# Attention block on one core: half of x transposed by DMA, contraction in chunks of 128, K in four tiles, the last projection beside the last unit, row bounds from bits

## The chip, the core and the metric

The kernel runs on one core of a Trainium2 chip. The core has a matrix engine (TensorE, PE in the profile), a vector engine (VectorE, DVE), an engine for element functions (ScalarE, ACT), a general engine (GpSimd, POOL) and one that mostly issues transfers (SyncE, SP). They run side by side, each through its own instructions in order, and wait for each other by semaphores. Matrix products land in PSUM, eight banks of 128 rows by 512 numbers of 32 bits; everything else lies in SBUF. Transfers are issued by SP, ACT or POOL and carried out by 16 DMA engines that all issuers share. The metric is the time of one execution on the device in microseconds (us).

## The reference

Input x has 2048 rows of 448 numbers in bf16. The weights wqkv make queries, keys and values of it, for 16 heads of 28 numbers each; wo projects the result back.

```python
qkv = (x @ wqkv).reshape(B, S, 3, H, Dh).transpose(2, 0, 3, 1, 4)   # B=1, S=2048, H=16, Dh=28
q, k, v = qkv[0], qkv[1], qkv[2]
scores = einsum("bhqd,bhkd->bhqk", q, k) * Dh ** -0.5
p = softmax(scores, axis=-1)
o = einsum("bhqk,bhkd->bhqd", p, v)
out = o.transpose(0, 2, 1, 3).reshape(B, S, D) @ wo
```

So there are 16 x 2048 x 2048 exponentials, 67 million, and they are the bulk of the element work.

## The kernel before

**Layout.** The 16 heads are taken in four groups g of four. A head takes 32 rows: 28 of data and four spare ones. XT holds x transposed, in four blocks of 512 rows, with the 448 columns as four chunks of 112 on the partitions (CK, line 83). WP holds the weights of one group, padded from 28 to 32 columns a head (pad_w, line 193, on DVE). QA is Q transposed for a group and a chunk c of 512 queries; KA is K transposed for a group, one tile of 2048 columns (line 116); VA is V with columns of ones, so that the product with V also gives the softmax's denominator in row 28.

**Tiles and units.** A tile (g, c, j, i) is 128 keys by 512 queries of one head. There are 1024; three in a row make a unit, 342 in all, the last with one tile only. The scores of a unit go to three PSUM banks, in turn spA and spB (emit_S, line 788). ACT takes the exponential of the unit in one instruction (emit_exp, line 806, L808). For some units ACT takes two tiles and DVE the third: DVE makes an exponential out of the score's bits (class Pair: bits at L825 for each tile, then mant, expo, square, line and rest for two tiles together), in three summands. PE multiplies each with V and sums over the keys in the bank o_ps (emit_wave, line 860, L871). A set is one group and one chunk of queries, 16 in all.

**The bound.** So that no exponential overflows, each row of scores is lowered by a bound, |q| max|k|. It sits in spare rows of QA, against rows of 1 and -1 in KA. For it, squares of K are summed over a head by a matmul with a mask (k_norm_mm, line 222) and reduced to a maximum (k_norm_max, line 225: four times a group, then once more over the four). q_root (line 256) makes the root on ACT, as a logarithm and an exponential of half of it (lz at L258, root at L260), and SP copies it into the row 31 of each head of QA, one transfer a chunk. For the first chunk the bound is made by separate instructions (lines 331 to 347).

**The start** (lines 134 to 349). SP loads x in four blocks and the greater part of the weights, ACT the weights of the first group. Nine matmuls on zeros warm PE up. PE transposes all of x by the identity (L292, 16 a block), DVE and ACT copy the results out of PSUM (evac_x, L298), then follow K of the first group, the norms and the first chunk of Q. The order is written out by hand.

**The middle.** From line 375 on a planner written in Python decides the order when the program is built. It steps through time with fixed durations (DUR, EXP_STEP), has one list of candidates per engine (pick_a, pick_p, pick_v), chooses which units give a tile to DVE (choose_d), and hands PE further tasks in gaps: K, Q, V and norms of the next group (k_task, kn_task, q_task, qn_task, v_task), and the output projection of finished rows (oproj_task, L491). Tasks use the bank misc. The resulting log is emitted in order; in_program_order keeps every engine to it.

**The end.** Once all scores are issued and the second last exponential is done, emit_fin (line 877) issues 12 matmuls (L883): the last 512 output rows, four blocks of 128, times the projection of the first three groups. Then come the last products with V, the division by the denominator in two halves (turned, line 911: transpose by 32 x 32 blocks, reciprocal, multiply, transpose back), the last group's projection (L974), copies out of PSUM and the stores.

**Row order.** Row r of x goes to partition r // 16 of the tiles (`x3 = x2.rearrange("(p t) c -> p t c", t=NKT)`), and the output's rows in the same way (out_perm); attention does not depend on the order of keys.

## Time and profile before

| | |
|---|---|
| median of 3 runs | 427.89 us (426.48 to 428.4) |
| profiled execution, time | 425.97 us |
| profiled execution, span | 424.2 us, first to last instruction |
| mean granted TensorE clock | 0.978 |
| first exponential (L808) starts | 19.93 us |
| last exponential (L808) starts, lasts | 412.68 us, 0.93 us |
| ACT busy from 60 to 120 us | 59.97 us |
| DVE busy from 60 to 120 us | 59.39 us |
| bits instructions on DVE (L825) | 170, mean 0.69 us |

All numbers but the median come from one profiled execution. A span counts from the first instruction to the last; the execution's time is a little longer. Where a line of the profile reads "L808 ACT ACTIVATE pt<-spA 128x1536 ... x171 | 243.0, 1421 | 4.2 <-PE spA L791 4.2", the engine ACT executed 171 instructions of line 808, which read tile spA and wrote pt, were busy for 243.0 us in all, 1421 ns each on average, and ACT stood idle 4.2 us just before them, for most of it until PE's instruction of line 791 was done. Lines of one instruction after another on ACT overlap: an exponential of 1536 columns lasts 1.45 us or more, and the next one starts 1.34 us after it. In the chain of waits, a line has the start, the length and what the end hung on at that time; "x4" are four instructions in a row. A waits line reads: who waited, for whom, us in total, times, longest.

### The profile page before, as it was taken

What the parts mean: (1) busy time and instruction counts of PE and PEld (TensorE: products, weight loads), DVE (VectorE), ACT (ScalarE), POOL (GpSimd) and SP (SyncE); (2) the same over time, 40 slices, a digit from 0 to 9 for tenths busy, and PEclk for the clock granted to TensorE, in tenths of its full rate; (3) what the DMA queues carried; (4) which work ended last, traced back from release to release, by engine and by line L of the source; (5) the groups of instructions that cost most, each with busy time, mean ns of one, the idle gap of its engine ahead of it and who ended that gap; (6) DMA issues with size and microseconds to landing.
All of it is one profiled execution on the core that took longest, in us unless ns stands there. A gap on an engine that the chain in (4) does not pass through costs nothing.

```text
span 424.2 us, 7645 instructions
## 1 busy us (share of the span) xinstructions
PE 352.1 (83%) x2968; PEld 126.1 (30%) x2968; DVE 387.3 (91%) x808; ACT 402.7 (95%) x366; POOL 4.4 (1%) x26
## 2 busy tenths in 40 slices
PE   8588888887888888888788888888897888898883
PEld 5243222222333222223333222222323322222221
DVE  4758999999999999999999999999989999999943
ACT  4599999999999999999999999999999999999991
POOL 4000000000000000000000000000000000000000
PEclk9989999999999999999999999999869999999997
DMA  8300000000000000000000000000000000001011
GB/s 247 80 0 3 2 23 5 2 27 0 14 17 26 2 4 25 2 25 2 29 2 19 10 1 27 1 15 14 29 2 3 25 1 23 24 11 34 11 34 43
DMA packets 10923, 9.16 MB, mean 22 GB/s; under 512 B 4940, under 2 KB 8840, under 8 KB 10888
## 3 DMA queue, kind: packets, MB, share of 16 engines
q1 hardware_dynamic: 9672, 8.25, 6.6%
q10 hardware_dynamic: 1216, 0.44, 0.4%
q8 instruction: 23, 0.38, 0.4%
q14 instruction: 12, 0.10, 0.1%
HBM read 6.59 MB, written 1.93 MB: 20 GB/s over the span
## 4 chain that ended last, share of the span: by engine, by line
ACT 66%; issue 14%; PE 11%; DVE 8%; ACTq 0%
ACT pt L808 64%; PE o_ps L871 3%; DVE bits L825 2%; PE spA L791 1%; PE spB L791 1%; PE K L301 1%; ACT lz L258 1%; DVE nsq L841 1%; PE K L202 1%; PE misc L268 1%; DVE rest L849 1%; ACT root L260 1%; DVE mant L830 1%; PE misc L234 1%; PE Ta L292 1%
## 5 line engine op out<-in xcount | busy, mean ns | idle before, releaser
L808 ACT ACTIVATE pt<-spA 128x1536 bf16<-128x1536 f32 (+1 forms) x171 | 243.0, 1421 | 4.2 <-PE spA L791 4.2
L808 ACT ACTIVATE pt<-spB 128x1024 bf16<-128x1024 f32 (+1 forms) x171 | 241.4, 1412 | 0.5 <-PE spB L791 0.5
L871 PE MATMUL o_ps<-pt,VA 128*32 128x512 bf16 x854 | 133.6, 391 | 0.2
L791 PEld LDWEIGHTS <-KA 32*128 32x128 bf16 x1024 | 51.7, 91 | 165.7 <-issue 122.1
L791 PE MATMUL spB<-QA,KA 32*128 32x512 bf16 x511 | 68.0, 385 | 31.2 <-ACT pt L808 27.9
L791 PE MATMUL spA<-QA,KA 32*128 32x512 bf16 x513 | 68.1, 387 | 30.9 <-ACT pt L808 24.7
L825 DVE TENSOR_SCALAR bits<-spB 128x512 int16<-128x512 f32 x86 | 59.0, 686 | 4.3 <-PE spB L791 3.1
L825 DVE TENSOR_SCALAR bits<-spA 128x512 int16<-128x512 f32 x84 | 57.6, 686 | 4.9 <-PE spA L791 3.9
L849 DVE TENSOR_TENSOR rest<-line,bits 128x1024 bf16<-128x1024 bf16 x85 | 57.8, 680 | 0.2
L841 DVE TENSOR_TENSOR nsq<-mant 128x1024 bf16<-128x1024 bf16 x85 | 57.9, 681 | 0.0
L871 PEld LDWEIGHTS <-VA 128*32 128x32 bf16 x1364 | 35.0, 94 | 71.8 <-issue 66.6
L871 PE MATMUL o_ps<-bits,VA 128*32 128x512 bf16 x170 | 54.0, 392 | 0.0
L871 PE MATMUL o_ps<-expo,VA 128*32 128x512 bf16 x170 | 37.0, 392 | 0.0
L830 DVE TENSOR_SCALAR mant<-bits 128x1024 int16<-128x1024 int16 x85 | 35.6, 418 | 0.2
L845 DVE TENSOR_SCALAR line<-nsq 128x1024 bf16<-128x1024 bf16 x85 | 35.4, 416 | 0.3
L835 DVE TENSOR_SCALAR expo<-bits 128x1024 int16<-128x1024 int16 x85 | 35.6, 419 | 0.0
L871 PE MATMUL o_ps<-rest,VA 128*32 128x512 bf16 x170 | 34.8, 396 | 0.0
L268 PEld LDWEIGHTS <-XT 112*128 112x128 bf16 x256 | 15.6, 101 | 11.9 <-issue 11.9
L268 PE MATMUL misc<-WRAW,XT 112*128 112x128 bf16 x208 | 18.8, 227 | 0.0
L234 PE MATMUL misc<-XT,WP 112*128 112x512 bf16 x60 | 18.5, 400 | 0.2
L238 DVE TENSOR_SCALAR QA<-misc,qmask,offs 128x512 bf16<-128x512 f32 x15 | 12.1, 805 | 4.0 <-PE misc L234 4.0
L202 PE MATMUL misc<-XT,WP 112*128 112x512 bf16 x48 | 14.3, 384 | 0.3 <-DVE KPART L226 0.3
(87 smaller groups left out, 195.4 us busy)
## 6 DMA issues: line engine op xcount, KB each, us to landing
rr<-scr SPq DMA_DIRECT2D x12, 256.0 KB
xs<-in_x_dram SPq DMA_DIRECT2D x4, 448.0 KB
out_dram<-osb SPq DMA_DIRECT2D x14, 112.0 KB
WRAW<-in_wqkv_dram SPq DMA_DIRECT2D x2, 290.5 KB
WRAW<-in_wqkv_dram SPq DMA_DIRECT2D x1, 392.0 KB
WO<-in_wo_dram SPq DMA_DIRECT2D x16, 24.5 KB
QA<-root SPq DMA_DIRECT2D x15, 4.0 KB
out_dram<-osb ACTq DMA_DIRECT2D x2, 112.0 KB
```

The source lines that it names most:

```text
L202: nc.tensor.matmul(out=ps, lhsT=WP[1][g][:, cc, :], rhs=XT[sc][:, cc, :], start=(cc == 0), stop=(cc == CC - 1))
L234: nc.tensor.matmul(out=ps, lhsT=WP[0][g][:, cc, :], rhs=XT[c][:, cc, :], start=(cc == 0), stop=(cc == CC - 1))
L268: nc.tensor.matmul(out=ps[:, t * P:(t + 1) * P], lhsT=XT[b][:, cc, t * P:(t + 1) * P], rhs=wcols(2, cc, g * HG, HG), start=(cc == 0), stop ...
L791: nc.tensor.matmul(out=sp[:, t * QW:(t + 1) * QW], lhsT=KA[g][HP * i:HP * (i + 1), j * P:(j + 1) * P], rhs=QA[g][c][HP * i:HP * (i + 1), : ...
L808: e = nc.scalar.activation(out=pt[:, 0:n * QW], in_=sps[u][:, 0:n * QW], func=ACT.Exp, scale=LN2, bias=-BIAS * LN2)
L825: return nc.vector.tensor_scalar(out=self.bits[:, k * QW:(k + 1) * QW], in0=ps, scalar1=0.0, scalar2=128.0, op0=ALU.max, op1=ALU.mult)
L830: nc.vector.tensor_scalar(out=self.m[:], in0=self.bits[:], scalar1=0x7F, scalar2=0x3F80, op0=ALU.bitwise_and, op1=ALU.bitwise_or)
L835: nc.vector.tensor_scalar(out=self.e[:], in0=self.bits[:], scalar1=0x7F80, scalar2=None, op0=ALU.bitwise_and)
L841: nc.vector.tensor_tensor(out=self.q[:], in0=m, in1=m, op=ALU.mult)
L845: nc.vector.tensor_scalar(out=self.l[:], in0=self.q[:], scalar1=CB, scalar2=CE, op0=ALU.mult, op1=ALU.add)
L849: nc.vector.tensor_tensor(out=self.c[:], in0=self.l[:], in1=self.bits[:].bitcast(BF16), op=ALU.mult)
L871: nc.tensor.matmul(out=o_cur[s][HP * i:HP * (i + 1), :], lhsT=VA[g][j // XB][:, j % XB, HP * i:HP * (i + 1)], rhs=rhs, start=(first_pv[(s, ...
```

## The change

- **x.** Blocks 2 and 3 of x (rows 1024 to 2047) are no longer loaded and transposed by PE. Two DMA transposes for each write XT directly (load_xt): one for columns 0 to 383 and one for columns 320 to 447. They stand on SP's queue behind the loads of blocks 0 and 1. Rows of blocks 0 and 1 are spread over the partitions as before, those of blocks 2 and 3 lie in natural order, in the output too (out_rows).
- **Chunks of 128.** The four chunks begin at columns 0, 128, 256 and 320. The last overlaps the third by 64, and the first 64 rows of its weights are zero (three memsets on POOL). Each load of weights is split in two transfers. WO is loaded by 4 transfers instead of 16.
- **K.** KA is four tiles of 512 columns per group. In the start, K1 and K2 are copied out by ACT (k_evac_act), and the steps of the start stand in a new order.
- **Bounds.** The root is made on DVE from the bits of the squared norms (q_bits): half of the sum of two numbers' bits is about the bits of the root of their product. KBITS adds half of the bits of max|k|^2 and a constant that keeps the bound high enough. The norms of K of groups 1 to 3 go to one bank by four matmuls, with one maximum and four tiny DVE steps (transpose of 32 x 32 blocks, maximum, scale, transpose back) for four maxima.
- **End.** The first two of the four last blocks get their projection of three groups in banks of the last unit's own tile, once all scores are issued and the exponential two before the last is done; the other two after the last product with V. The division transposes once in full and then works in two halves; ACT copies three blocks out, DVE one.

The two orders of instructions on the engines differ in number as follows: bits 168 for 170, with 84 pairs for 85; maxima of norms in the middle (KPART and kt from misc) 3 for 12; transposes of x on PE 32 for 64; transfers issued by ACT at the start 4 for 2; by SP up to and with WO 16 for 23.

```diff
+WARM2 = 0
-    CK = D // CC
+    CK = 128
+    C3 = D - CK
+    CEIL = 12.0
+    MINUS_ROOT = 0.5 * 127 * 2.0 ** 23 + 0.0435 * 2 ** 23 - 2.0 ** 31
...
-    KA = [big.tile([P, S], BF16, name=f"KA{g}") for g in range(2)] * 2
+    KA = [[big.tile([P, QW], BF16, name=f"KA{g}_{c}") for c in range(NQC)] for g in range(2)] * 2
...
     def load_w(t, eng, a, b):
-        eng.dma_start(out=WRAW[t][:, :, a:b], in_=wq3[:, :, t * D + a:t * D + b])
+        cols = slice(t * D + a, t * D + b)
+        eng.dma_start(out=WRAW[t][:, 0:CC - 1, a:b],
+                      in_=wqkv[0:(CC - 1) * CK, cols].rearrange("(cc p) n -> p cc n", p=CK))
+        eng.dma_start(out=WRAW[t][CK // 2:CK, CC - 1, a:b], in_=wqkv[D - CK // 2:D, cols])
...
+    def load_xt(b, eng):
+        rows = x2[b * QW:(b + 1) * QW]
+        eng.dma_start_transpose(out=XT[b][:, 0:CC - 1, :], in_=rows[:, 0:(CC - 1) * CK])
+        eng.dma_start_transpose(out=XT[b][:, CC - 1:CC, :], in_=rows[:, C3:D])
+
+    for t in range(3):
+        nc.gpsimd.memset(WRAW[t][0:CK // 2, CC - 1, :], 0.0)
     load_x(0, nc.sync)
     load_w(1, nc.scalar, 0, W0)
     load_x(1, nc.sync)
     load_w(0, nc.scalar, 0, W0)
-    load_x(2, nc.sync)
-    load_x(3, nc.sync)
+    load_xt(2, nc.sync)
+    load_xt(3, nc.sync)
     load_w(2, nc.sync, 0, D)
     load_w(1, nc.sync, W0, D)
     load_w(0, nc.sync, W0, D)
...
+    nc.gpsimd.memset(kt[0][:], 0.0)
+    nc.gpsimd.memset(kt[2][:], 0.0)
...
-    def q_root(ps, g, cs):
-        lz = wk.tile([P, QW], F32, name="lz")
-        nc.scalar.activation(out=lz[:], in_=ps, func=ACT.Ln, bias=epscol[:, 0:1], scale=KMAX2[g][:, 0:1])
-        su = wk.tile([P, QW], BF16, name="root")
-        nc.scalar.activation(out=su[:], in_=lz[:], func=ACT.Exp, scale=0.5)
+    def q_bits(ps, g, cs):
+        su = wk.tile([P, QW], I16, name="root")
+        nc.vector.tensor_scalar(out=su[:], in0=ps.bitcast(I32), scalar1=2.0 ** -17, scalar2=KBITS[g][:, 0:1],
+                                op0=ALU.mult, op1=ALU.add)
...
+    def k_bits(g):
+        nc.vector.tensor_scalar(out=KBITS[g][:], in0=KMAX2[g][:, 0:1].bitcast(I32), scalar1=2.0 ** -17,
+                                scalar2=CEIL, op0=ALU.mult, op1=ALU.add)
...
+        def k_evac_act(ps, sc):
+            nc.scalar.activation(out=KA[0][sc][:], in_=ps, func=ACT.Identity, scale=kmask[:, 0:1], bias=ones[:, 0:1])
...
         pad_w(nc.vector, 1, 0)
         transposes(1)
         evac_x(1)
+        pad_w(nc.vector, 0, 0)
         k_mm(bank["K0"], 0, 0, ALLC)
         k_sq_act(bank["K0"], 0, 0)
-        pad_w(nc.vector, 0, 0)
-        transposes(2)
-        evac_x(2)
         k_evac(bank["K0"], 0, 0)
         k_mm(bank["K1"], 0, 1, ALLC)
         k_sq_act(bank["K1"], 0, 1)
-        transposes(3)
-        evac_x(3)
+        q_mm(bank["Ta0"], 0, 0, ALLC)
+        q_sq_act(bank["Ta0"], 0, 0)
+        k_norm_mm(bank["Tb0"], 0, 0)
+        k_norm_max(bank["Tb0"], 0, 0)
         k_mm(bank["K2"], 0, 2, ALLC)
...
-        nc.scalar.activation(out=lk[:], in_=KMAX2[0][:], func=ACT.Ln, bias=epscol[:, 0:1])
-        nc.scalar.activation(out=ak[:], in_=lk[:], func=ACT.Exp, scale=0.5)
...
-        k_evac(bank["K2"], 0, 2)
+        k_evac_act(bank["K1"], 1)
+        k_evac_act(bank["K2"], 2)
         k_evac(bank["K3"], 0, 3)
...
-    for h in range(H):
-        g, i = divmod(h, HG)
-        nc.sync.dma_start(out=WO[HP * i:HP * i + Dh, g, :], in_=wo[h * Dh:(h + 1) * Dh, :])
+    for i in range(HG):
+        nc.sync.dma_start(out=WO[HP * i:HP * i + Dh, :, :],
+                          in_=wo.rearrange("(g i e) n -> i e g n", g=G, i=HG)[i])
...
+            red = add_v(lambda: nc.vector.reduce_max(out=kt[0][:, 0:1], in_=tk.tile[:], axis=AX.X), "kred", [mm_], 2)
+            steps_ = [lambda: nc.vector.transpose(out=kt[1][:], in_=kt[0][:]),
+                      lambda: nc.vector.reduce_max(out=kt[3][:], in_=kt[1][:, Dh:HP], axis=AX.X),
+                      lambda: nc.vector.tensor_scalar(out=kt[2][:, Dh:HP], in0=kt[3][:].to_broadcast([P, NQC]),
+                                                      scalar1=MARG2, scalar2=None, op0=ALU.mult),
+                      lambda: nc.vector.transpose(out=kt[4][g][:], in_=kt[2][:])]
...
-            op = Op(lambda: q_root(tk.tile[:], g, cs), 0, [mm] + [("kmax", g, sc) for sc in range(NQC)] * (g > 0))
-            alist.append(op)
+            kb = add_v(lambda: k_bits(g), "tiny", [("kmax", g)] if g else [], 3, margin=0.03)
+            op = add_v(lambda: q_bits(tk.tile[:], g, cs), "evac", [mm, kb], 2)
...
     def emit_fin():
-        fin = sp_tile(NU)
-        fin_banks.extend([fin[:, 0:QW], fin[:, QW:2 * QW], fin[:, 2 * QW:3 * QW], misc_tile()[:]])
-        for tq in range(XB):
-            for g in range(G - 1):
-                nc.tensor.matmul(out=fin_banks[tq][:, 0:D], lhsT=OT[g][CL][:, tq * P:(tq + 1) * P],
-                                 rhs=WO[:, g, :], start=(g == 0), stop=False)
+        sp = sps[NU - 1]
+        fin_banks.extend([sp[:, QW:2 * QW], sp[:, 2 * QW:3 * QW]])
+        for tq in range(2):
+            fin_mm(tq)
+
+    def fin_mm(tq):
+        for g in range(G - 1):
+            mm = nc.tensor.matmul(out=fin_banks[tq][:, 0:D], lhsT=OT[g][CL][:, tq * P:(tq + 1) * P],
+                                  rhs=WO[:, g, :], start=(g == 0), stop=False)
+            if tq < 2:
+                beside.append(mm)
...
     o_ps = o_cur[NSET - 1]
+    last = sp_tile(NU)
+    fin_banks.extend([last[:, 0:QW], last[:, QW:2 * QW]])
+    fin_mm(2)
+    fin_mm(3)
     half = QW // 2
-    for k in range(2):
-        for f in turned(last_g, CL, lambda: o_ps, slice(k * half, (k + 1) * half)):
-            f()
+    nc.vector.transpose(out=oT[:], in_=o_ps[:])
+    nc.vector.reciprocal(out=rT[:], in_=oT[:].rearrange("p (b e) -> p b e", e=HP)[:, :, Dh])
...
```

## The prediction

> **What bounds the kernel now.** I read the busy shares first, then ScalarE (ACT) by groups and by waits, then the chain of waits in order of time at both ends, then the DMA traffic of the first 10.6 us. From the page, the busy lines:
>
> ```profile
> PE 352.1 (83%) x2968; PEld 126.1 (30%) x2968; DVE 387.3 (91%) x808; ACT 402.7 (95%) x366; POOL 4.4 (1%) x26
> ```
>
> Busy time by stretch, for the 60 us from 60 (columns: PE, PEld, DVE, ACT, POOL, granted clock, DMA share, GB/s):
>
> ```profile
> 60.00:120.00 60.00, 50.82 (x435) 17.80 (x435) 59.39 (x122) 59.97 (x55) 0.00 (x0) 1.00 0.05 15
> ```
>
> In the middle ACT has no gap, and VectorE (DVE) nearly none. ACT's waits, and two of its groups:
>
> ```profile
> ACT osb L983 <- PE spA L974: 6.1, 1, 6.1
> ACT pt L808 <- PE spA L791: 4.2, 4, 3.0
> ...
> L258 ACT ACTIVATE lz<-misc,epscol,KMAX 128x512 f32<-128x512 f32 x4 | 3.9, 963 | 0.0
> L260 ACT ACTIVATE root<-lz 128x512 bf16<-128x512 f32 x4 | 2.5, 630 | 0.1
> ```
>
> So the exponentials (L808) are the clock of the kernel: the first starts at 19.93 and the last (412.68 + 0.93) ends at 413.61. The time has three stages: 19.93 us before, 393.7 us with ACT full, 10.6 us after. The change touches all three. The chain of waits shows what sets the first and the last:
>
> ```profile
> 13.14 0.86 PE K L202 x4
> ...
> 14.26 1.90 DVE KPART L226 x3
> 16.16 0.02 issue
> 16.18 0.16 DVE KMAX L228
> 16.34 0.72 DVE qt L343
> ...
> 17.16 0.75 DVE QA L346
> 17.91 1.45 DVE KA L206 x2
> ...
> 33.80 0.66 ACT lz L258
> ...
> 413.17 1.86 PE spA L883 x9
> 415.03 0.57 PE misc L883 x3
> 415.60 0.38 PE o_ps L871 x4
> ```
>
> The first score matmul waits for the last write of K, 1.45 us after Q is ready. At the end twelve matmuls of the output projection (2.4 us) stand in PE's queue ahead of the four that finish the attention.
>
> **The change, stage by stage. The start.** In the chain PE is continuous from 1.19 to 14.0. The nine warm-up matmuls end at 5.20; x0 lands by 4.81 and is loaded as before. Removed from PE: 32 of 64 transposes, 16 per block, 0.90 us a block. Removed behind the last K: the two K copies ahead of the scores (1.45), since K now lies in four tiles and the first scores read tile 0 alone; the two tiny ACT steps lk and ak and the wait for them (16.38 to 16.98); and qt (0.72), which moves ahead of the last two maxima. Added: Q's matmuls ahead of K2, and two K copies on ACT (0.6 each by ksq, L219). New schedule on the old durations: transposes 5.20 to 7.67, K0 8.53, K1 9.39 (its second half waits for ACT's copy at 8.72), Q 10.25, one norm matmul 10.47, K2 11.33, two norm matmuls 11.77, K3 12.63. DVE: maximum 0 by 11.55, maximum 1 by 12.63, qt 13.43, maxima 2 and 3 by 14.8, then 0.16 + 0.15 + 0.75 to QA at 15.9. First scores 15.95 to 16.35. ACT has lq and aq until 14.75, then the two copies until 15.95, so it is free in time. First exponential at 16.4, a gain of 3.5, if the transposed blocks are there: block 2 by 10.47, block 3 by 11.77.
>
> That is the one unknown price. The order of issue shows that block 3's first transpose waits for the semaphore of the first K weights, so SP and everything behind it (all later weights, WO) stand until these land, which is by 6.70, when the padding copy L197 runs without a wait. The trace of before has no DMA transpose. Bounds by pieces: a block is 512 rows in four chunks, 2,048 pieces of 256 B. The DMA traffic from 0 to 10.6 us (packets, MB, share of 16 engines):
>
> ```profile
> q1 hardware_dynamic: 1296, 2.41, 78.1%
> q10 hardware_dynamic: 928, 0.21, 10.2%
> ```
>
> The cheap end is a plain load of the same bytes: x1 is there by 6.57, 1.76 us behind x0, and nothing is held. The nearest row is q10, with pieces of 226 B: 10.2% of 16 x 10.6 us over 928 is 18.6 ns each, so 2.4 us a block; block 2 lands at about 6.5 + 2.4 = 8.9, block 3 at 11.3, and nothing is held, though by half a microsecond only. The costly end is the mean packet of the SP queue over the whole page (6.6% of 16 x 424.2 us over 9,672 = 46 ns): 5.9 us a block, block 3 at 18.3, 6.5 us late. I take q10's row, nearest in size, and 0.5 us for the thin margin: **-3.0 us**; ends -3.5 and +3.0.
>
> Other edits of the start. POOL gets three memsets of 64 x 452 (0.40 each, by WO's 1.59 us for 1,792 columns) and two small ones ahead of the identity, some 1.4 us: identity 1.31 to 2.8 (needed at 5.2), ones 3.07 to 4.7 (needed at 9.2), WO's memset 5.1 to 6.6; covered by the warm-ups and the x load. ACT issues four loads instead of two (0.42 to 0.52 each), about 1 us ahead of its table load, which then ends by 4.0; its first copy is at 6.72. SP issues three more weight loads and twelve fewer of WO. Six weight loads at 0.92 each (2.75 / 3) after block 3's issue at about 7 end at 12.5, and landing four later (x0: 0.74 to 4.81) makes 16.6. The padding copies of group 1 stand on DVE just there, at 16.7, and behind them Q's next evacuation, whose bank PE needs; before, that evacuation had 2.22 us to wait anyway (L238), so up to 2 us late is free. W2, first of the six, is wanted by PE at 18.4 and lands near 12.
>
> [...]
>
> [...]
>
> **The middle.** q_root leaves ACT: lz and root cost 33.80 to 35.12 in the chain, 1.32 us, four times: -5.28. The order of instructions has 168 bits instructions on DVE for 170, so two exponentials are 1536 wide instead of 1024. Steps in the timeline are 1.34 (310.56 to 311.90) and 0.90 (309.66 to 310.56): +0.87. Sum **-4.4**. ACT's own waits inside this stage are under 2 us and the planner is the same; I leave them. Is DVE able to follow? Out: 12 maxima at 0.68 (8.2), three KMAX at 0.16 (0.5), one pair of shares (2 x 0.69 + 0.42 + 0.68 + 0.42 + 0.68 + 0.42 = 4.0), together 12.7. In: three maxima (2.0), four square-root evacuations at 0.80 as L238 (3.2), and 16 tiny ones between 0.15 (L345) and 0.20 (L902 is 0.24 at the far end), 2.4 to 3.8. Net -3.7 to -5.1 on 371 us, the same share as ACT. The added wait: the root evacuation sits in DVE's order behind KBITS and the last maximum, and SP's copies of its rows behind it; the tasks of a group are spread to end six units (BGEND, 6 x 1.34 = 8 us) ahead of its first score, which leaves room for a landing like x0's (4.1). Cost taken 0; between -1 (DVE's relief) and +4.4 (all of it lost to DVE).
>
> **The end.** Counted from 413.61 in the old trace. Two of the four last row blocks get their six projection matmuls beside the last unit, the others after the last attention matmul. That matmul then starts at 413.7 and not 415.53, ends by 414.05. DVE: one transpose 0.71, reciprocal 0.24, then twice 0.43 + 0.45, with gaps 416.9. The other six matmuls run under the first transpose. Last two matmuls, 0.7, to 417.65. ACT copies blocks 0 and 1 from 416.75 (0.53 each) since their tile is no longer shared, then block 3 until 418.35; DVE block 2 until 418.27. Issue 0.40, and landing as before (421.72 to 424.2, 2.5): 421.3. **-2.9 us**; ends -1.8 (the queue alone, 415.53 to 413.7) and -3.3.
>
> Sum: -3.0 - 4.4 - 2.9 = -10.3. Profiled execution 425.97 (span 424.2) to 415.7; it ran 1.92 under the median 427.89, and against that median I predict **417.6 us**.
>
> **Rivals.**
> 1. The transposes are late but not ruinous: 46 ns a piece, block 3 at 18.3, first exponential 22.9. -4.3 in all: 423.6. For it: from 4 to 12 us the DMA share is 1.0 to 1.2, so pieces queue. Against: fewer bytes are ahead of them.
> 2. DVE becomes the bound, as it takes the root: the middle gives nothing back, 422.0. For it: 59.39 of 60. Against: the count above.
> 3. Other side. The transposes hold SP and K3 together. Break-even is block 3 at 11.8 + 10.8 = 22.6 us, some 63 ns a piece. The q1 row of the first 10.6 us has 102 ns a packet (1.86 KB each); at that price the blocks take 26.1 us, K3 starts at 32.6, the first exponential is at 37.2, 17.3 later than before; with -4.4 and -2.9 that is 437.9, and W2 and the padding weights stand behind. Against: 256 B is an eighth of that packet.
> 4. The first scores still wait for all of K, by a dependence that the split does not cut: 1.4 us of the start is lost, 419.0; the order shows waits on tile 0 alone.
>
> **How the numbers follow.** Forecast (with 4) 0.64, rival 1 0.13, rival 2 0.10, rival 3 0.09, gains that cancel 0.04. Rivals 1 and 2 are still faster: faster 0.87, same 0.04, slower 0.09. About 0.5% is what a measurement of this kernel can tell from no change. The range goes down to 414.5 (ends -3.5, -5.4, -3.3 make 415.7, and a run a quarter per cent low) and up to 424.0, which holds rivals 1 and 2.
>
> **What the profile after would show.** First L856 exponential near 16.4; K2 and K3 matmuls without an idle before them put down to DMA XT; no lz or root on ACT after the start; DVE no fuller than 59 of 60; the last exponential to the end 7.7 us instead of 10.6; the last attention matmul right after the last exponential. Wrong if a DMA wait stands before K2 or K3 for over 3 us, if ACT shows idle time on PE scores in the middle beyond 3 us, or if PE's projection still precedes the last attention matmul.

## The result, and the profile after

The changed kernel takes 421.31 us (median of 4 runs, 419.91 to 422.63), the kernel before, run beside it on the same chip, 427.93 us (426.48 to 428.4). The ratio is 0.985, with a 95% interval from 0.981 to 0.989: faster by 1.5%. The forecast was 417.6 us with a range of 414.5 to 424.0.

The profiled execution of the changed kernel took 422.0 us (span 420.1), against 425.97 (span 424.2) before. Cut into the three stages of the prediction:

| stage | before | after | difference | predicted |
|---|---|---|---|---|
| start, to the first exponential | 19.93 | 17.09 | -2.84 | -3.0 |
| middle, to the end of the last exponential | 393.68 | 395.33 | +1.65 | -4.4 |
| end | 10.59 | 7.68 | -2.91 | -2.9 |

Two stages came as predicted. The middle, which should have given the most, gave nothing back between these two executions. From the page after, the busy lines:

```profile
PE 349.0 (83%) x2909; PEld 121.4 (29%) x2932; DVE 379.6 (90%) x802; ACT 399.3 (95%) x357; POOL 5.8 (1%) x31
```

The busy time by stretch of 60 us (columns: PE, PEld, DVE, ACT, POOL, granted clock, DMA share, GB/s), after:

```profile
60.00:120.00 60.00, 48.85 (x420) 17.16 (x424) 58.39 (x122) 60.00 (x55) 0.00 (x0) 1.00 0.04 12
120.00:180.00 60.00, 51.90 (x426) 16.79 (x429) 55.75 (x117) 57.71 (x51) 0.00 (x0) 0.91 0.04 11
...
300.00:360.00 60.00, 49.91 (x415) 15.99 (x416) 55.47 (x112) 57.82 (x52) 0.00 (x0) 0.86 0.04 12
```

The same view of before, two of the same stretches:

```profile
120.00:180.00 60.00, 50.47 (x430) 17.39 (x430) 58.85 (x120) 60.00 (x55) 0.00 (x0) 1.00 0.04 11
300.00:360.00 60.00, 51.16 (x443) 18.06 (x440) 56.39 (x114) 58.93 (x54) 0.00 (x0) 0.92 0.04 14
```

Where the granted clock is 1.00, ACT is full after nearly as before (60.00 here, 59.35 from 180 to 240 us). Where it is 0.91 or 0.86, ACT idles for 2 us in 60. DVE is no fuller than 58.4 of 60, and less full where ACT idles. So it is not DVE that took the gain. ACT's waits after (who waited, for whom: us in total, times, longest):

```profile
ACT pt L856 <- PE spA L839: 3.4, 5, 1.0
ACT pt L856 <- PE spB L839: 3.4, 8, 0.9
ACT osb L1054 <- PE spB L1046: 3.2, 1, 3.2
```

In the same view of before, the prediction shows the row of spA (4.2 us, longest 3.0). The other one is:

```profile
ACT pt L808 <- PE spB L791: 0.5, 1, 0.5
```

Before, the exponentials waited 4.7 us for PE (4.2 for spA, 0.5 for spB), 3.0 of them ahead of the first one: 1.7 us inside the middle. Now they wait 6.8, of which 1.0 is ahead of the first: 5.8 us inside the middle, in twelve waits.

I took the middle apart by the start times of the exponentials in the trace. Where nothing is late, the next one starts 1.332 us after the start of one of 1536 columns, and 0.904 us after one of 1024. What a step takes beyond that is a loss; four steps of before hold the root and are counted by themselves. The parts sum to the stretch from the first exponential's start to the last one's:

| | steps at their usual length | roots on ACT | loss at half clock | loss elsewhere | sum |
|---|---|---|---|---|---|
| before | 381.45 | 6.15 | 2.57 | 2.57 | 392.75 |
| after | 382.31 | 0 | 8.78 | 3.37 | 394.46 |

The rest of the +1.65 is the last exponential itself, shorter by 0.06. "At half clock" means that the step ends in, or up to 2.5 us after, a stretch in which TensorE's granted clock is 0.5; such stretches come in multiples of 3.41 us (3.41, 6.83 and 10.24 us in these two traces). In the middle they add up to 13.7 us before and 34.1 us after. The loss is larger than ACT's idle time, since an exponential lasts 1.45 us and its successor may start at 1.332: a small lateness shows in the steps alone.

The page's row of the granted clock in 40 slices (tenths of full speed, 9 is 0.9 or more) shows where, before:

```profile
PEclk9989999999999999999999999999869999999997
```

and after:

```profile
PEclk9899999999979899999999998999889879999998
```

### The profile page after: what moved, and what is told of

It is laid out like the page before. It is cut to its first block, busy times and chain, and to the rows that moved or that the text cites. A ratio compares the mean times of both kernels' runs of the same rounds, so it can differ in the third digit from the quotient of the medians.

```text
span 420.1 us, 7576 instructions
## 1 busy us (share of the span) xinstructions
PE 349.0 (83%) x2909; PEld 121.4 (29%) x2932; DVE 379.6 (90%) x802; ACT 399.3 (95%) x357; POOL 5.8 (1%) x31
## 4 chain that ended last, share of the span: by engine, by line
ACT 61%; issue 18%; PE 13%; DVE 6%; DMA 2%; ACTq 0%; DVEq 0%
ACT pt L856 60%; PE o_ps L922 4%; PE spB L839 3%; PE spA L839 2%; DMA WRAW<-in_wqkv_dram 2%; DVE bits L876 1%; PE misc L298 1%; PE misc L259 1%; DVE rest L900 1%; DVE QA L263 1%; PE o_ps L298 0%; DVE nsq L892 0%; DVE mant L881 0%; PE K L227 0%; DVE root L285 0%
## 5 line engine op out<-in xcount | busy, mean ns | idle before, releaser
L856 ACT ACTIVATE pt<-spA 128x1536 bf16<-128x1536 f32 (+1 forms) x171 | 246.8, 1443 | 3.7 <-PE spA L839 3.4
L856 ACT ACTIVATE pt<-spB 128x1024 bf16<-128x1024 f32 (+1 forms) x171 | 230.5, 1348 | 3.6 <-PE spB L839 3.4
L839 PEld LDWEIGHTS <-KA 32*128 32x128 bf16 x1024 | 50.1, 91 | 166.5 <-issue 123.0
L876 DVE TENSOR_SCALAR bits<-spB 128x512 int16<-128x512 f32 x102 | 69.9, 686 | 8.3 <-PE spB L839 7.4
L876 DVE TENSOR_SCALAR bits<-spA 128x512 int16<-128x512 f32 x66 | 45.4, 687 | 10.5 <-PE spA L839 9.9
L922 PE MATMUL o_ps<-expo,VA 128*32 128x512 bf16 x168 | 38.7, 411 | 0.2 <-DVE expo L886 0.2
L922 PE MATMUL o_ps<-rest,VA 128*32 128x512 bf16 x168 | 36.8, 406 | 0.0
L298 PEld LDWEIGHTS <-XT 128*128 128x128 bf16 x256 | 16.0, 102 | 12.4 <-issue 12.2
L298 PE MATMUL misc<-WRAW,XT 128*128 128x128 bf16 x208 | 19.1, 228 | 0.5 <-DVE root L285 0.4
L259 PE MATMUL misc<-XT,WP 128*128 128x512 bf16 x55 | 16.6, 391 | 0.8 <-issue 0.7
L227 PE MATMUL misc<-XT,WP 128*128 128x512 bf16 x41 | 13.2, 389 | 0.0
```

Source lines behind the costliest of these rows:

```text
L259: nc.tensor.matmul(out=ps, lhsT=WP[0][g][:, cc, :], rhs=XT[c][:, cc, :], start=(cc == 0), stop=(cc == CC - 1))
L298: nc.tensor.matmul(out=ps[:, t * P:(t + 1) * P], lhsT=XT[b][:, cc, t * P:(t + 1) * P], rhs=wcols(2, cc, g * HG, HG), start=(cc == 0), stop ...
L839: nc.tensor.matmul(out=sp[:, t * QW:(t + 1) * QW], lhsT=KA[g][j // XB][HP * i:HP * (i + 1), (j % XB) * P:(j % XB + 1) * P], rhs=QA[g][c][H ...
L856: e = nc.scalar.activation(out=pt[:, 0:n * QW], in_=sps[u][:, 0:n * QW], func=ACT.Exp, scale=LN2, bias=-BIAS * LN2)
L876: return nc.vector.tensor_scalar(out=self.bits[:, k * QW:(k + 1) * QW], in0=ps, scalar1=0.0, scalar2=128.0, op0=ALU.max, op1=ALU.mult)
L922: nc.tensor.matmul(out=o_cur[s][HP * i:HP * (i + 1), :], lhsT=VA[g][j // XB][:, j % XB, HP * i:HP * (i + 1)], rhs=rhs, start=(first_pv[(s, ...
```

## The experiments

Three questions were put: whether the level of the clock is a matter of chance or of the kernel, what in the kernel sets it, and whether start and end came out right for the reasons given.

**The kernel before again, and the root back on ACT.** The first run is the kernel before, unchanged. The second is the changed kernel with q_root on ACT again:

```diff
...
-            kb = add_v(lambda: k_bits(g), "tiny", [("kmax", g)] if g else [], 3, margin=0.03)
-            op = add_v(lambda: q_bits(tk.tile[:], g, cs), "evac", [mm, kb], 2)
+            op = Op(lambda: q_root(tk.tile[:], g, cs), 0, [mm] + [("kmax", g)] * (g > 0))
+            alist.append(op)
```

> The kernel before, unchanged, profiled once more. In the two profiles at hand the middle (first exponential to last) has 13.7 us at half the TensorE clock before and 34.1 us after; ACT loses 2.6 us against its full steps in these stretches before and 8.8 us after, about 0.26 us for each us at half clock. Clock theory: the middle of this run is 387.6 us (steps and roots) plus 2.6 plus 0.26 times its time at half clock; as the median is 2 us over the first profile, I expect some 20 us at half clock and 394 to 396 us. Plan theory (the clock does not matter, the order of the plan makes the waits): 393.7 us whatever the clock is.

> After, with the root back on ACT (logarithm and exponential, four times), all else as after. First theory (moving the root gave ACT its time back, and something else took it): the roots cost four times 1.5 = 6.1 us again and two units more have a share on DVE (-0.9), so the middle is 5.3 us longer than after at an equal time at half clock, 400 to 401 us, and the time 426.5. Rival (the root moved to DVE costs what it gave, DVE being the bound): the middle stays within 1 us of 395.3 and the time at 421 to 422.

The kernel before against itself: 428.56 us (10 runs, 424.33 to 429.71) beside 426.94, ratio 1.003 (1.000 to 1.006). Its profiled execution had a span of 428.0, 3.8 us more than the one that the prediction was made from, with the same instructions. Its loss is 9.16 us instead of 5.14, and 6.13 of it lies in 22.9 us at half clock. From the start of the first exponential to that of the last it takes 396.52 us instead of 392.75. The clock theory gives 396.2 for 22.9 us at half clock; the plan theory forecast no change.

Its ten runs go from 424.33 us at a mean clock of 0.992 to 429.71 at 0.969; 0.023 of clock over 428 us are 19.7 us more at half clock, so each costs some 0.27 us. Over all 43 executions of this kernel in these experiments, with one and the same order of instructions, the span runs from 422.5 to 428.0 us and grows by 0.23 us for each us at half clock (2 x span x (1 - mean clock); correlation 0.93). So the clock moves the time with the plan unchanged. The profile that I read before predicting was one of the better executions of that kernel: against the second one, whose middle lasts 397.45 us to the end of the last exponential, the changed kernel's 395.33 would be a gain of 2.1 us.

With the root back on ACT the time is 425.88 us (ratio to before 0.9945, 0.991 to 0.998), by the ratios some 4 us more than the changed kernel. Its middle is 397.87 us to the end of the last exponential, less than the 400 to 401 forecast, as its loss is 9.6 us where the changed kernel's is 12.2. In its profile the four steps with a root are 1.40, 1.60, 1.61 and 1.35 us longer than usual, 5.96 in all, and this row is back:

```profile
L293 ACT ACTIVATE lz<-misc,epscol,KMAX 128x512 f32<-128x512 f32 x4 | 3.7, 922 | 0.0
```

So the move of the root was worth what the prediction gave it, and a little more (5.28 predicted; 6.15 and 5.96 measured).

**More and fewer filler matmuls.** The planner gives PE a matmul on data that nobody uses where its estimate of the array's use is below SHARE (0.36). The two runs change only that number, to 0.48 and to 0:

```diff
-SHARE = 0.36
+SHARE = 0.48
```

> After, with the planner's threshold for filler matmuls raised from 0.36 to 0.48: 47 filler matmuls instead of 27, 168 shares on DVE as in after. Clock theory: fewer stretches of 3.4 us with little work on PE, at most 15 us at half clock in the middle instead of 34, ACT waits for PE scores under 4 us instead of 6.8, time 416 to 418. Plan theory: ACT waits as in after, 421 us; or slower by what 20 more matmuls take on PE (20 x 0.21 = 4 us at most), 425.

> After, with no filler matmuls at all (threshold 0), 168 shares on DVE. Clock theory: 60 us or more at half clock in the middle, at 0.26 us each 7 us more of waiting on ACT than after: 428 us or more. Plan theory: PE has 27 matmuls less (5.8 us) and fewer conflicts: 420 to 421.

With 47 fillers instead of 27: 421.6 us (420.19 to 423.56), clock 0.953 to 0.965, half clock in the middle 36.9 us. That is no gain, and the forecast of the clock theory failed here. With none: 422.83 us (422.12 to 429.42), clock 0.917 to 0.945, 59.3 us at half clock and a loss of 15.25, 13.31 of it there. The clock theory had the clock right and the time wrong (428 or more); by its ratio of 0.988 (0.984 to 0.993) this kernel is not told apart from the changed one. PE has 27 matmuls less in it; what they give back was not measured by itself. Fewer fillers lower the clock; more of them, put where this planner puts them, do not raise it.

**The bundled norms of K.** The change gathers four norms of a group in one task; that leaves other gaps on PE. One run undoes this part in the changed kernel, the other does it alone in the kernel before. The first of the two, in part:

```diff
-    def kn_task(rel, g):
...
-        tasks.append(Task(rel, [("ksq", g, sc) for sc in range(NQC)], cut(mm, NQC, [2, 2]), after))
+    def kn_task(rel, g, sc):
+        def after(tk, mm):
+            return [add_v(lambda: k_norm_max(tk.tile[:], g, sc), "red", [mm], 2, ("kmax", g, sc))]
+        tasks.append(Task(rel, [("ksq", g, sc)], [(1, lambda ps: k_norm_mm(ps, g, sc))], after))
```

> After, with the norms of K in groups 1 to 3 as before: twelve tasks of one matmul and one maximum, spread over the group, instead of three of four matmuls. The first call of runs showed that the TensorE clock falls to half behind 3.4 us windows in which the matmuls use under about a third of the array; after has 14 such windows in the middle (under 0.34) and before 6. Bundle theory: the bundling took single matmuls out of the thin windows, so undoing it gives the clock back: granted clock 0.970 to 0.980, 15 to 20 us at half clock in the middle, 417 to 418.5 us although only 166 tiles are DVE's (+0.9). Rival (the plan's thin windows come from elsewhere): clock 0.95 to 0.967 as in after, 421 to 422.5 us.

> Before, with only the bundling of K's norms taken over from after (root on ACT, chunks of 112, all of x transposed by PE, end as before); 170 shares on DVE as in before, 22 filler matmuls for 27. Bundle theory: granted clock falls from 0.968 to 0.985 to 0.945 to 0.965, 12 to 15 us more at half clock, 0.25 us each: 430 us. Rival: clock and time as before, 426 to 428 us.

Undone in the changed kernel: 420.92 us, ratio 0.9895 (0.983 to 0.996), clock 0.944 to 0.969. No difference that these runs can tell, and the forecast of the bundle theory failed. Done alone in the kernel before: 436.28 us, ratio 1.021 (1.013 to 1.029). It does less work on DVE, has five filler matmuls less, and is 2% slower. Its clock row:

```profile
PEclk9999999999959999999985899997959989889997
```

It has 58.0 us at half clock in the middle and a loss of 15.85 us, 14.27 of it there. So the same part costs 2% in one kernel and nothing in the other: it is not the cause by itself, but it moves the plan, and another plan can have another clock.

**What a plan does to the clock.** In every trace I added up, in the 3.41-us units of the clock's own record, the part of the array that the matmuls use: each one's length at full clock, times its rows and columns over 128 (in the changed kernel's K, one matmul of 512 columns starts 0.216 us after another). A product with scores uses 32 rows (`32*128` in the timelines) and one with V 32 columns (`128*32`), so a quarter each; a projection uses all (`128*128`). The kernels' means in the middle lie between 0.44 and 0.48, but the thin units differ (the counts move by up to three with the way in which a matmul on the border of two units is counted):

| kernel | units under 0.34 | half clock in the middle, us | loss, us |
|---|---|---|---|
| before | 6 | 13.7 | 5.1 |
| before, second profile | 6 | 22.9 | 9.2 |
| after | 14 | 34.1 | 12.2 |
| root on ACT | 13 | 30.7 | 9.6 |
| more filler | 10 | 36.9 | 13.3 |
| no filler | 20 | 59.3 | 15.3 |
| single norms | 9 | 21.9 | 7.7 |
| before, norms bundled | 14 | 58.0 | 15.9 |

Each row is one profiled execution; that of after was the second slowest of its four, that of the single norms the fastest. The plan of after's middle stands, instruction for instruction, in three more profiles below (x on PE, the earlier copies, the end put back): they have 30.6, 23.8 and 50.4 us at half clock, losses of 10.3, 9.1 and 14.1 us, and 9 to 16 thin units. So the level goes with the plan, and each execution has its share of chance in it.

The thin units come first and the half clock after them. Over all fourteen profiles, of 26 units at full clock with less than 0.30 of the array used 22 were followed by half clock, of 209 from 0.30 to 0.38 some 40, and of 1237 with 0.38 or more a single one. PE's busy share on the page (83%) tells nothing of this: a matmul that uses a quarter of the array is as busy as one that uses all of it (on the page after, of 512 columns each, 395 ns for scores and 403 ns with V beside 389 ns in K and 391 ns in Q). To tell cause from company I changed one size of the plan: into how many tasks the projection of V for a group is cut. I did it once in the direction that leaves few thin stretches in the plan (four tasks, shown here), and once, as a control, in the other (`VP = [2, 2]`). The work stays but for two things that the planner does by itself: it places 30 and 33 fillers instead of 27, and with V in twos it gives DVE two tiles less, which is worth 0.86 us:

```diff
-VP = [1, 1, 2]
+VP = [1, 1, 1, 1]
```

> The changed kernel with one size of the plan changed: the projection of V for a group is cut into four tasks of one block each instead of three of one, one and two (VP). The plan then has, by its own list of matmuls, 1.6% of all stretches of 3.41 us with less than 0.32 of the array used, where the changed kernel has 5.4% and the kernel before 1.4%; its modelled waits of ScalarE are 3.9 us instead of 5.7. Theory A (the middle lost time because its matmuls leave more thin stretches, which the half clock follows): clock 0.97 to 0.98, half clock in the middle 12 to 20 us instead of 34, loss of the middle 7 to 9 us instead of 12.2, time 416 to 418.5. Rival B (the clock falls by chance from run to run, or with the total of the work, which is the same): clock 0.955 to 0.965 as before the edit, time 419.5 to 421.5. Rival C (the loss is ScalarE's waits that the planner models): 1.8 us less, time 419.5, at the same clock.

> The control: the same size changed the other way, V's projection in two tasks of two blocks. The plan moves as much, its modelled waits are 4.7 us (the changed kernel 5.7), but the share of stretches of 3.41 us below 0.32 of the array is 5.8%, as in the changed kernel (5.4%). Theory A: clock 0.95 to 0.965, half clock in the middle 30 us or more, time 420 to 422.5. Rival C (modelled waits): 420.3. If any other plan is better than the changed kernel's (theory D, its plan is simply unlucky): clock near 0.975 and time 416 to 418.

V in fours: 416.07 us (415.14 to 419.07), ratio to before 0.976 (0.972 to 0.980), clock 0.974 to 0.990, 6 thin units, 19.7 us at half clock, loss 8.9. V in twos: 419.59 us, ratio 0.985 (0.981 to 0.988), the same as the changed kernel, clock 0.958 to 0.968, 8 thin units, 27.0 us, loss 8.1.

By the ratios, the same work cut in another way thus gives some 4 us in one direction and nothing in the other, and time and clock go with the thin stretches that the plan showed. The forecasts in us came from a set of runs with the kernel before at 427.93; here it took 425.71, so I read them as ratios to it. On V in fours theory A (0.972 to 0.978) holds; the chance theory (0.980 to 0.985) and the modelled waits (0.980) lie just outside the interval in time, and fail clearly in the clock, which both left unchanged. On V in twos the time fits theory A (0.981 to 0.987) and the modelled waits (0.982) alike, with 27.0 us at half clock where theory A had 30 or more.

The two profiles alone would not have shown the gain: that of V in fours has the larger loss. Over the four executions of each, though, both kernels lie on straight lines of span against half clock that meet at the same 411 us at full clock, so the clock is enough to part them. The clock row of V in fours, from its profiled execution, the slowest of its four:

```profile
PEclk9898999999999999989998999999996999999999
```

**The start: x transposed by PE, and the copies of K.** In one run all of x is loaded as rows and transposed by PE (load_x and transposes for blocks 2 and 3 again); in the other the copies of K1 and K2 stand earlier on ACT, ahead of the squares of K2 and of K3, and K3's copy goes from DVE to ACT:

```diff
-    load_xt(2, nc.sync)
-    load_xt(3, nc.sync)
+    load_x(2, nc.sync)
+    load_x(3, nc.sync)
...
+        transposes(2)
+        evac_x(2)
...
+        transposes(3)
+        evac_x(3)
```

and

```diff
         k_mm(bank["K2"], 0, 2, ALLC)
+        k_evac_act(bank["K1"], 1)
         k_sq_act(bank["K2"], 0, 2)
...
         k_mm(bank["K3"], 0, 3, ALLC)
+        k_evac_act(bank["K2"], 2)
         k_sq_act(bank["K3"], 0, 3)
...
-        k_evac_act(bank["K1"], 1)
-        k_evac_act(bank["K2"], 2)
-        k_evac(bank["K3"], 0, 3)
+        k_evac_act(bank["K3"], 3)
```

> After, with all four blocks of x loaded as rows and transposed by PE, chunks of 128 and everything else as in after, the same plan. Theory that the DMA transposes give the start its PE time: 32 transposes more, 1.8 us, in a chain that already waits 0.6 us for the weights of Q; first exponential 1.2 to 1.8 us later than in after, 18.3 to 18.9 us. Rival (the start's gain comes from the moved K copies and steps, the transposes hold SP and delay the weights as much as they save): first exponential at 17.1 or earlier.

> After, with the copies of K1 and K2 on ACT ahead of the squares of K2 and K3, and K3 copied by ACT at the end and not by DVE behind Q. In after the first scores started at 16.61, 0.15 behind the copy of K3 (15.65 to 16.46) and 0.87 behind Q (15.74), though they read K0 alone. Theory that they wait for every read of the first stage's PSUM banks, so that splitting K cut nothing: with the copies early the scores start 0.15 behind Q, at 15.9 to 16.0, and the first exponential at 16.4. Rival (the first scores wait for something else, PE's loads or the warm clock): first exponential at 17.1 as in after.

With x on PE the first exponential starts at 18.30 instead of 17.09: by this pair the DMA transposes are worth 1.2 us of the start's 2.84, and the other edits of the start together the rest. But the start is not the same in every execution: in seven other profiles whose start is that of the changed kernel the first exponential comes at 17.09 to 17.77, so that the transposes are worth between 0.5 and 1.2 us. With the earlier copies it starts at 16.66 (418.82 us in a single run, clock 0.971), earlier than in any of these. The timeline of the changed kernel (start, length, engine, line, instruction, in brackets the idle time before it and what ended it):

```profile
10.38 1.03 PE L227 MATMUL K<-XT,WP 128*128 128x512 bf16 x4
...
11.68 1.03 PE L227 MATMUL K<-XT,WP 128*128 128x512 bf16 x4
...
14.99 0.75 DVE L376 SCALAR_TENSOR_TENSOR QA<-su,nk,qt 128x512 bf16<-128x512 f32 x1
15.65 0.81 DVE L231 TENSOR_SCALAR KA<-K,kmask,ones 128x512 bf16<-128x512 f32 x1
...
16.61 0.39 PE L839 MATMUL spA<-QA,KA 32*128 32x512 bf16 x3 [2.84 <-DVE KA L231]
```

K2 and K3 start without a wait for a transfer. But the first scores wait until DVE's copy of K3 is done (16.46), though they read tile 0 alone. With the earlier copies:

```profile
15.28 0.75 DVE L378 SCALAR_TENSOR_TENSOR QA<-su,nk,qt 128x512 bf16<-128x512 f32 x1
...
16.18 0.39 PE L839 MATMUL spA<-QA,KA 32*128 32x512 bf16 x3 [2.12 <-DVE QA L378]
```

Now they follow QA. The likely reason for the old wait is that the score banks take the place of the first stage's banks (ps0, L312, closed before psum, L388, opens), so they wait for the last reader of any of them; that this is the dependence was not tried by itself.

**The end put back.** The changed kernel with emit_fin, the division and the last stores of before (all twelve matmuls of the last four blocks at once, after the last unit's scores):

```diff
...
-        sp = sps[NU - 1]
-        fin_banks.extend([sp[:, QW:2 * QW], sp[:, 2 * QW:3 * QW]])
-        for tq in range(2):
-            fin_mm(tq)
...
+        fin = sp_tile(NU)
+        fin_banks.extend([fin[:, 0:QW], fin[:, QW:2 * QW], fin[:, 2 * QW:3 * QW], misc_tile()[:]])
+        for tq in range(XB):
+            for g in range(G - 1):
+                nc.tensor.matmul(out=fin_banks[tq][:, 0:D], lhsT=OT[g][CL][:, tq * P:(tq + 1) * P],
+                                 rhs=WO[:, g, :], start=(g == 0), stop=False)
...
```

> The changed kernel with only its end put back: all four blocks of the last projection wait for the last unit, in one tile of their own and the misc tile, and the last four outputs go out one after the other as before. The plan of the middle is the same. Theory: from the end of the last exponential to the end of the span 10.4 to 10.7 us as in the kernel before, instead of 7.7; time 424 at the clock of the changed kernel (0.955 to 0.965). Rival (the shorter end comes from the chunks of 128 rows and not from the projection beside the unit): 7.7 to 8.5 us.

One run, 427.04 us with a clock of 0.933 and 50.4 us at half clock in the middle, more than expected for the plan of the changed kernel, which it shares. The stage itself is clear: from the last exponential's end (414.58) to the end of the span (425.2) 10.6 us, as before. Its timeline, the two projections ahead of the last products with V:

```profile
413.71 0.87 ACT L858 ACTIVATE pt<-spB 128x512 bf16<-128x512 f32 x1
414.14 1.86 PE L936 MATMUL spA<-WO,OT 128*128 128x448 bf16 x9 [0.44 <-ACT pt L858]
415.84 0.73 PE L936 MATMUL misc<-WO,OT 128*128 128x448 bf16 x3
416.50 0.40 PE L924 MATMUL o_ps<-pt,VA 128*32 128x512 bf16 x4
416.98 0.45 DVE L974 STREAM_TRANSPOSE oT<-o_ps 128x256 f32<-128x256 f32 x1 [3.65 <-PE o_ps L924]
```

Here oT starts 2.40 us after the last exponential's end. The chain of waits of the changed kernel (start, length, what the end hung on):

```profile
410.64 0.37 PE spB L839
411.01 1.24 PE spB L937 x6
412.25 0.77 PE o_ps L922 x8
413.01 0.02 issue
413.04 0.73 DVE oT L1035
```

There the last exponential ends at 412.42 and oT starts at 413.04, 0.62 us later.

**A version that beats both.** The start of the earlier copies, V in fours, and three more sizes of the plan, chosen by the thin stretches that the plan shows:

```diff
-DCON = 2.2
+DCON = 2.0
-AGE = 2.0
+AGE = 1.5
-SHARE = 0.36
+SHARE = 0.38
-VP = [1, 1, 2]
+VP = [1, 1, 1, 1]
...
```

> The start of e8_k_copies_early (all copies of K but the first on ScalarE) with the plan of VP in four, AGE 1.5 instead of 2.0, DCON 2.0 instead of 2.2 and SHARE 0.38 instead of 0.36: stretches below 0.32 of the array 0.5%, modelled waits 3.9 us. Theory A: clock 0.98 or more, half clock in the middle under 14 us, loss under 7 us, time 413.5 to 416. Rival B: what e8_k_copies_early gives, 418.8 at a clock of 0.96 to 0.97.

415.34 us (413.96 to 416.22), ratio to before 0.9746 (0.971 to 0.978), clock 0.987 to 0.998. By the ratio it is not told apart from V in fours. Three thin units, 3.4 us at half clock, loss 4.8, of which 3.5 lies elsewhere, as in the changed kernel (3.4). Its clock row:

```profile
PEclk9999999999899999999999999999999999999998
```

Its span, 413.1, is 7.0 under that of the changed kernel: start -0.7, middle -7.3 (from first to last exponential 387.12 instead of 394.46), end +1.0. The end is longer because here PE has the six matmuls of L937 at 404.45, ahead of the last products with V at 405.68, whereas the last exponential ended at 404.40; that microsecond was left.

## Why the prediction was right and where it was not

- **The start, -3.0 forecast, -2.84 measured: the sum right by luck, its parts not.** QA was ready at 15.74, where the schedule said 15.9, and the transposed blocks held nothing up: K2 and K3 started at 10.38 and 11.68, where 10.47 and 11.77 were forecast. So rivals 1 and 3 are out, and the 0.5 us kept for late transposes was not needed. The trace's DMA records show the landing: 4096 packets of 256 B, as many as the prediction counted, run from 4.92 to 10.83 us, and half of them are done by 8.33, where 8.9 and 11.3 were forecast. At 21.9 ns a packet they cost a little more than the 18.6 taken from q10's row; that is 1.05 MB in 5.9 us, or 177 GB/s, beside the weights' packets. The split weight loads held up little: of the padding copies of group 1, the one that had to wait for its weights waited 0.20 us. What filled the 0.5 us was the wait of rival 4, which the prediction had all but set aside because "the order shows waits on tile 0 alone". The split of K cut nothing: the scores stood until the end of K3's copy, 0.72 us after QA. Rival 4 priced this at 1.4, both copies; it cost 0.72, since ACT made two of the three copies beside QA. Without it (the earlier copies), 16.66 comes near the nominal 16.4.
- **The end, -2.9 forecast, -2.91 measured: right, and for the reason given.** With the queue of twelve matmuls ahead of the last products with V, the division and the stores put back, the stage is 10.6 again. The queue is 1.78 us of it (oT starts 2.40 us after the last exponential with it and 0.62 without), as the prediction's nearer end of 1.8 had it; the rest comes behind oT and was not taken apart.
- **The root, -5.28 forecast, and the two wider exponentials, +0.87.** Measured -6.15 and +0.86 (382.31 less 381.45). A root costs more than the two instructions, 1.54 on average for 1.32.
- **DVE as the new bound (rival 2).** The time of the middle is what this rival forecast, no gain at all, but not its mechanism: DVE was at 58.4 of 60 where ACT was full, and less where ACT waited, and the waits are on PE.
- **The step that failed** is "ACT's own waits inside this stage are under 2 us and the planner is the same; I leave them". The planner was the same, its plan was not: with other tasks, the changed kernel's profile has 14 thin units where that of before has 6, TensorE's clock is halved for 34.1 us instead of 13.7, and the loss grows from 5.14 to 12.15 us. The +7.0, less the root's extra 0.9, is the difference between -4.4 and +1.65. Part of it is the choice of executions: the two profiles of before have a mean loss of 7.2, the four with the changed kernel's plan one of 11.4, so that 4.3 us is the better size of the term that was left at nothing. The prediction's own sign of being wrong, ACT idle on PE's scores in the middle beyond 3 us, is there with 5.8. That the clock moves with the plan while the work stays is shown by V in fours, and by the last version, whose start differs too; that it can go the other way, by the kernel before with bundled norms. The profile of before had the sign: at 20 us and in two stretches between 300 and 317 us it has half the clock, and nearly all of ACT's idle time in the middle lies there or just behind. I read that row as a property of the chip and not of the plan. The idle time of under 2 us was read rightly, but by the exponentials' starts the loss was 5.14 us even there.
- **The total.** By the stages of the two profiles the change gave 4.1 us; by the medians, 6.6, as the profiled execution of before was 1.96 under its median and that of after 0.7 above its own. The range held it, since its upper part was there for transposes and DVE; the mechanism that used it was not among the rivals, so that the time lay within the range is luck.

In the profiles of before and after, every half-clock stretch in the middle is a multiple of 3.41 us long (nine stretches, of 3.41, 6.83 or 10.24 us). The first of each kernel, at 20.0 and 17.9 us, comes behind the 4.10 and 2.84 us that PE waited for the first scores; the other seven come without such a wait: the longest idle time of PE in the middle is 1.0 us before and 1.3 us after, and by the records PE is busy in 83% of the time. By the count over the fourteen profiles, all but one of the some 63 units that half clock followed had less than 0.38 of the array used, and 22 of them less than 0.30.

## What to carry to other kernels

Work taken off the engine that bounds a kernel comes back as a gain only if the plan of the other engines stays as good (here 6.15 us of roots went and 7.0 us of loss came); when a planner lays the work out anew, read its result (here the array's use in stretches as short as the clock's unit), not its rules. Before reading a difference of 1% from two profiles, put the time lost at a lower granted clock into a column of its own, and take the profile of the kernel before twice. A tile split to shorten a wait may leave the wait as it was, as the split of K did here: look at who the first reader really waits for.

## What the runs showed of the hardware

- Half clock costs less than one would think where PE is not the bound: over the fourteen profiles (with those of x on PE, the earlier copies, V in fours and in twos, the end put back and the last version beside those of the table) the loss grows by 0.21 us for each us at half clock in the middle (a straight line through them, correlation 0.96). Within the kernel before alone, over 43 executions, it is 0.23.
- Half clock follows thin work and not only idle time (seven of the nine stretches of before and after come with no idle time on PE over 1.3 us): 22 of 26 units below 0.30 of the array, and 1 of 1237 at 0.38 or more, were followed by it. It is a tendency and no sharp bound: in the changed kernel units at 0.33 of the array occur without half clock after them (at 103 and 107 us). What sets it off stays open.
- The DMA transposes held their issuing queue. In the timeline of the changed kernel, SP's rows of issue:

```profile
1.66 2.49 SPq L152 DMA_TRANSPOSE XT<-in_x_dram  x1
...
4.20 1.68 SPq L153 DMA_TRANSPOSE XT<-in_x_dram  x1
...
5.92 2.26 SPq L152 DMA_TRANSPOSE XT<-in_x_dram  x1
...
8.22 1.26 SPq L153 DMA_TRANSPOSE XT<-in_x_dram  x1
...
9.53 0.58 SPq L143 DMA_DIRECT2D WRAW<-in_wqkv_dram  x1
```

  A transpose of 512 x 384 took 2.3 to 2.5 us of the queue and one of 512 x 128 1.3 to 1.7, against 0.40 to 0.59 for the plain loads on the same queue, so that SP was taken for 7.8 us and the later weights were issued from 9.5 on. What stood behind them was not wanted before 16 us, and the only wait for it in the start is one of 0.20 us.
